# Matmul operands on multiples of 512 bytes, and a convolution tile without zero columns

## The chip, the cores and the metric

One NeuronCore of one Trainium2 chip runs the whole program. The metric is the device time of that core in microseconds (us), the median of the runs. TensorE (PE) multiplies, VectorE (DVE), ScalarE (ACT) and GpSimd (POOL) do the elementwise work, and SyncE (SP) issues the loads and stores. SBUF is the on-chip memory with 128 partitions; PSUM holds matmul results.

## What is computed

Two batches of 768 tokens go through three blocks, all in fp32. The first is a windowed attention with block summaries; the other two are dense. Cut to what matters here:

```python
# block 2: x is (2, 768, 512); w_in (512, 1024); w_spatial (768, 768)
h = np.maximum(x @ w_in, 0.0)
u, v = h[..., :512], h[..., 512:]
v_n = (v - mean(v)) / np.sqrt(var(v) + 1e-06)
v_s = np.einsum('ts,bsd->btd', w_spatial, v_n) + b_spatial[None, :, None]
x = (u * v_s) @ w_out                      # (2, 768, 512)
# block 3: w_in (512, 1024), conv_w (3, 1024), w_out (1024, 512)
h = np.maximum(x @ w_in, 0.0)
hp = zero_row, h, zero_row                 # along the 768 tokens
conv = sum(conv_w[k] * hp[:, k:k + 768, :] for k in range(3))
return (h * sigmoid(conv)) @ w_out
```

## The kernel before

Every dense product is made of fp32r parts: `split` (lines 66 to 73) writes a value as a high and a low half, and `mm3` (lines 58 to 64) adds up three matmuls for each 128 rows of the contraction: high by high (line 62), high by low (line 63) and low by high (line 64). In `PE.matmul` the first operand, `lhsT`, is the stationary one (128 columns, loaded into the array as weights), and `rhs` is the moving one (384 or 512 columns, streamed through).

After the attention, whose order is written out by a planner (`Plan`, lines 133 to 173), the dense stages follow each other (lines 610 to 620); there the framework's scheduler fixes the order on each engine when the program is built, from its own model of the times. Their tiles in the profile, in order:

- `f1v` (tile vps, 512 columns, 144 matmuls): stationary x, moving w1. `f1u` (ups, 384 columns): stationary w1, moving x.
- `spatial` (sps, 384 columns, 288 matmuls): stationary vn, moving wsp.
- `merge_weights` (wps, 512 columns, 96 matmuls): stationary wo, moving wi. It multiplies the two weight matrices between the blocks, once.
- `i2(b)` (hps, 384 columns, 192 matmuls for each batch b): stationary wp, moving g1. Its 8 steps f make h, the convolution and the gate.
- `o2(b)` (ops): stationary y, moving w2. For each batch 6 row tiles by 8 steps f by 3 matmuls, which makes 144. The last row tile of the second batch is done in two halves of 256 columns, so that 264 of the 288 have 512 columns and 48 have 256.

Where the operands lie: tiles are placed one after another in each partition, pool by pool, and every tile is rounded up to 32 bytes. The program's own constants and the pools `const` and `slots` end on a multiple of 512 bytes, and every tile of `slots` (w1, w2, wi, x, g1, vn, wp, u) begins on one. The pool `tmp` takes 5 tiles of 2048 bytes, 5 of 32 (bs) and 5 of 32 (mv): 10,560 bytes, which is 20 times 512 and 320 more. So the attention's pool and, after it in the same place, the pool `late` begin 320 bytes past a multiple of 512. In `late`, the 6 tiles of the tag S (6144 bytes, 12 times 512: wsp, later y) lie at 320; the 3 tiles of the tag T (line 604; 2 by 770 floats, 6160 bytes, placed 6176 apart) lie at 320, 352 and 384; the two Y tiles (y of f = 6 and 7) at 416. The stationary wo lies in T tiles (line 446, cut into units of 2048 bytes by `units`). So three kinds of dense operand lie off a multiple of 512: the moving wsp, the stationary wo and the stationary y.

The convolution (lines 476 to 497) works on one T tile for each f: in its first half hh, 770 columns wide, a zero column (DVE, lines 480 and 481), 768 columns of h that ACT writes from PSUM in two parts (line 486), and a zero column; in its second half ct. ACT writes the first tap (line 487), DVE adds the second and the third (line 489), ACT takes the sigmoid (line 490), POOL multiplies by h (line 491), and `split` writes y: its high half by ACT (line 70), its low half by POOL in batch 0 and by DVE in batch 1 (line 73). A T tile is free for step f + 3 when y of step f is written.

Of the kernel before, what the change touches and what calls it, by code (L numbers as in the profile page):

```python
# [11 lines left out]
F32 = mybir.dt.float32  # L12
F32R = mybir.dt.float32r
BF16 = mybir.dt.bfloat16
U32 = mybir.dt.uint32
AF = mybir.ActivationFunctionType
ALU = mybir.AluOpType
# [3 lines left out]
B, H, S, D = 2, 8, 768, 64  # L21
# [14 lines left out]
HS = S // 2  # L36
# [3 lines left out]
def block_kernel(ctx, tc, q_in, k_in, vwin, v_in, mask, runs, w_in, w_spT, b_sp, w_outT, w_in2, conv, w_out2, out):  # L40
    nc = tc.nc
    PE, DVE, ACT, POOL, SP = nc.tensor, nc.vector, nc.scalar, nc.gpsimd, nc.sync

    const = ctx.enter_context(tc.tile_pool(name="const", bufs=1))
    slots = ctx.enter_context(tc.tile_pool(name="slots", bufs=1))
    tmp = ctx.enter_context(tc.tile_pool(name="tmp", bufs=5))
    psm = ctx.enter_context(tc.tile_pool(name="psm", bufs=2, space=PSUM))

    mm_pools = [psm, None, 0]
# [2 lines left out]
    def mmps(name):  # L52
        mm_pools[2] += 1
        if mm_pools[1] and mm_pools[2] % 2:
            return mm_pools[1].tile([128, 512], F32, tag="o", name=name)
        return mm_pools[0].tile([128, 512], F32, tag="mm", name=name)

    def mm3(ps, pairs, first=True, last=True):

        n = len(pairs)  # L60
        for i, ((lh, ll), (rh, rl)) in enumerate(pairs):
            PE.matmul(ps, lhsT=lh, rhs=rh, start=first and i == 0, stop=False)  # L62
            PE.matmul(ps, lhsT=lh, rhs=rl, start=False, stop=False)  # L63
            PE.matmul(ps, lhsT=ll, rhs=rh, start=False, stop=last and i == n - 1)  # L64

    def split(src, hi, lo, heng=None, leng=None):

        heng, leng = heng or ACT, leng or POOL
        if heng is ACT:
            ACT.copy(hi, src)  # L70
        else:
            heng.tensor_copy(hi, src)
        leng.tensor_tensor(out=lo, in0=src, in1=hi.bitcast(F32), op=ALU.subtract)  # L73
# [40 lines left out]
    conv_t = const.tile([128, DF // 128 * 3], F32, name="conv_t")  # L114
# [213 lines left out]
    vn, u, g1, wsp = {}, {}, {}, []  # L328
# [92 lines left out]

    def load_wsp():
        for t in range(NT):
            wsp.append(late.tile([128, 2, S], F32R, tag="S", name=f"wsp_{t}", bufs=6))
            st = t_slot(f"wst_{t}", F32)[:, 0, :S]
            SP.dma_start(st, w_spT[t * 128:(t + 1) * 128, :])
            split(st, wsp[t][:, 0], wsp[t][:, 1], leng=POOL if t % 2 else DVE)
# [17 lines left out]
    def load_wo():  # L445
        wm["o"] = units(lambda n: t_slot(n, F32R), "wo", 8)
        for c in range(4):
            load_weight(w_outT[c * 128:(c + 1) * 128, :], wm["o"][2 * c], wm["o"][2 * c + 1], f"wot_{c}")
            yield
# [20 lines left out]
    def wp(c, hf):  # L470
        return wm["p"][8 * hf + 2 * c], wm["p"][8 * hf + 2 * c + 1]


    y, w2 = {}, {}

    def i2(b):
        for f in range(8):
            tt = t_slot(f"hh_{b}_{f}", F32)
            hh, ct = tt[:, 0], tt[:, 1, :S]
            DVE.memset(hh[:, 0:1], 0.0)  # L480
            DVE.memset(hh[:, S + 1:S + 2], 0.0)
            for h in range(2):
                ps = mmps(f"hps_{b}_{f}_{h}")
                fs, hs = slice(f % 4 * 128, (f % 4 + 1) * 128), slice(h * HS, (h + 1) * HS)
                mm3(ps[:, :HS], [((wp(c, f // 4)[0][:, fs], wp(c, f // 4)[1][:, fs]), (g1[b, c][:, 0, hs], g1[b, c][:, 1, hs])) for c in range(4)])
                ACT.activation(out=hh[:, 1 + h * HS:1 + (h + 1) * HS], in_=ps[:, :HS], func=AF.Relu)
            ACT.activation(out=ct, in_=hh[:, 0:S], func=AF.Copy, scale=conv_t[:, 3 * f:3 * f + 1])  # L487
            for j in (1, 2):
                DVE.scalar_tensor_tensor(out=ct, in0=hh[:, j:j + S], scalar=conv_t[:, 3 * f + j:3 * f + j + 1], in1=ct, op0=ALU.mult, op1=ALU.add)  # L489
            ACT.activation(out=ct, in_=ct, func=AF.Sigmoid)  # L490
            POOL.tensor_tensor(out=ct, in0=hh[:, 1:S + 1], in1=ct, op=ALU.mult)  # L491
            if f < 6:
                y[b, f] = late.tile([128, 2, S], F32R, tag="S", name=f"y_{b}_{f}", bufs=6)
            else:
                y[b, f] = late.tile([128, 2, S], F32R, tag="Y", name=f"y_{b}_{f}", bufs=2)
            split(ct, y[b, f][:, 0], y[b, f][:, 1], heng=ACT, leng=DVE if b else POOL)
            yield

# [99 lines left out]
    late = ctx.enter_context(tc.tile_pool(name="late", bufs=2))  # L598
# [2 lines left out]
    raw_pool[0] = late  # L601

    def t_slot(name, dt):
        return late.tile([128, 2, S + 2], dt, tag="T", name=name, bufs=3)

    b_bc = late.tile([128, S], F32, name="b_bc", bufs=1)
    SP.dma_start(b_bc, b_sp.partition_broadcast(128))
    load_wsp()
    load_f64(conv, "conv", conv_t)
    run(f1v(0))  # L610
# [4 lines left out]
    run(spatial(1), load_wi(1))  # L615
    run(merge_weights())
    run(i2(0), load_w2())
    run(o2(0))
    run(i2(1))
    run(o2(1))  # L620

# [57 lines left out]
```

## Time and profile before

| | |
|---|---|
| median of 3 runs | 360.98 us (360.39 to 361.37) |
| profiled execution: span from the first to the last instruction | 358.8 us |
| its own time | not given beside the span; the median lies 2.18 us above the span |
| busy PE, DVE, ACT, POOL | 345.1, 229.4, 183.4, 157.9 us |

The profile is one execution. Busy time is a union of the records on an engine; matmuls overlap in their records, so a busy PE need not be a PE at its peak. How fast PE works in a stage is better read from the starts of its matmuls: the time between the first start of a stage and the first start of the next, by the number of matmuls in between. That is called the pace below.

### The profile page before, as it was taken

The page shows a single profiled execution, that of the slowest core. Times are in us where ns is not written, and L with a number is a line of the kernel's source. Part 1 is how long each engine was busy: PE and PEld are TensorE (multiplying, and loading weights), DVE is VectorE, ACT ScalarE, POOL GpSimd, SP SyncE. Part 2 cuts the span into 40 slices and gives each one's busy share as a digit, 9 for nine tenths or more (in the row PEclk, how much of TensorE's full clock was granted, in tenths as well). Part 3 has the DMA queues.
Part 4 walks back from the last instruction along what each step waited for, and adds up shares of the span by engine and source line. Part 5 has one row for each costly group of instructions (what it writes and reads, how often), then busy time and mean ns, then how long its engine had stood idle before and what let it go on. Part 6 is the DMA issues. An engine that isn't in the chain of part 4 may idle for free.

```text
span 358.8 us, 6400 instructions
## 1 busy us (share of the span) xinstructions
PE 345.1 (96%) x2487; PEld 301.0 (84%) x2487; DVE 229.4 (64%) x390; ACT 183.4 (51%) x374; POOL 157.9 (44%) x159
## 2 busy tenths in 40 slices
PE   8998899999797999999999999999999999999996
PEld 4766677777586999899999888999888899998885
DVE  3889998884179799779298899457620025886000
ACT  2766778757264442355342464867531047874101
POOL 3789999765136142116133062587870003333000
PEclk9999999999899899999999999999999999999999
DMA  8877888320381232015232351000002020000202
GB/s 259 276 231 239 235 265 248 98 68 2 94 293 43 58 103 74 0 35 164 97 107 71 108 166 78 2 0 0 2 0 88 2 88 1 3 0 2 88 0 88
DMA packets 11118, 33.86 MB, mean 94 GB/s; under 512 B 1488, under 2 KB 1872, under 8 KB 11088
## 3 DMA queue, kind: packets, MB, share of 16 engines
q1 hardware_dynamic: 11088, 33.46, 29.8%
q8 instruction: 19, 0.31, 0.3%
q14 instruction: 11, 0.09, 0.1%
HBM read 30.31 MB, written 3.15 MB: 93 GB/s over the span
## 4 chain that ended last, share of the span: by engine, by line
PE 86%; DVE 4%; DMA 3%; POOL 2%; issue 2%; ACT 1%; SPq 0%; POOLq 0%; ACTq 0%; DVEq 0%
PE ops L63 6%; PE ops L62 6%; PE ops L64 6%; PE hps L62 6%; PE hps L63 6%; PE hps L64 6%; PE sps L64 5%; PE sps L62 5%; PE sps L63 5%; PE xp L310 3%; PE s L284 3%; PE pt L305 3%; PE mm L247 2%; PE vps L62 2%; PE wps L64 2%; PE wps L63 2%
## 5 line engine op out<-in xcount | busy, mean ns | idle before, releaser
L489 DVE SCALAR_TENSOR_TENSOR hh<-hh,conv_t 128x768 f32<-128x768 f32 x32 | 43.2, 1349 | 41.9 <-ACT hh L487 41.4
L491 POOL TENSOR_TENSOR hh<-hh 128x768 f32<-128x768 f32 x16 | 25.4, 1588 | 53.7 <-ACT hh L490 53.7
L63 PE MATMUL hps<-g,wp 128*128 128x384 f32 x128 | 42.8, 334 | 0.0
L64 PE MATMUL hps<-g,wp 128*128 128x384 f32 x128 | 42.8, 334 | 0.0
L62 PE MATMUL hps<-g,wp 128*128 128x384 f32 x128 | 42.8, 334 | 0.0
L62 PE MATMUL ops<-w,y 128*128 128x512 f32 (+1 forms) x104 | 39.0, 377 | 0.0
L63 PE MATMUL ops<-w,y 128*128 128x512 f32 (+1 forms) x104 | 38.9, 377 | 0.0
L64 PE MATMUL ops<-w,y 128*128 128x512 f32 (+1 forms) x104 | 37.8, 376 | 0.0
L62 PE MATMUL sps<-wsp,vn 128*128 128x384 f32 x96 | 32.9, 343 | 1.8 <-ACT vn L382 1.8
L64 PE MATMUL sps<-wsp,vn 128*128 128x384 f32 x96 | 32.7, 345 | 0.5 <-DVE vn L385 0.5
L63 PE MATMUL sps<-wsp,vn 128*128 128x384 f32 x96 | 32.9, 343 | 0.0
L301 POOL TENSOR_TENSOR e<-e,st 128x480 f32<-128x480 f32 x24 | 25.4, 1061 | 15.6 <-DVE st L298 5.3
L292 ACT ACTIVATE e<-s,st 128x120 f32<-128x120 f32 x96 | 26.8, 371 | 7.2 <-DVE st L288 7.1
L517 ACT COPY o<-ops 128x512 f32<-128x512 f32 (+1 forms) x13 | 6.8, 557 | 40.0 <-PE ops L64 39.5
L62 PEld LDWEIGHTS hps<-g,wp 128*128 128x128 f32 x128 | 24.0, 188 | 0.1
L63 PEld LDWEIGHTS hps<-g,wp 128*128 128x128 f32 x128 | 24.0, 188 | 0.1
L64 PEld LDWEIGHTS hps<-g,wp 128*128 128x128 f32 x128 | 24.0, 188 | 0.0
L64 PEld LDWEIGHTS ops<-w,y 128*128 128x128 f32 x104 | 19.5, 188 | 4.0
L62 PEld LDWEIGHTS ops<-w,y 128*128 128x128 f32 x104 | 19.5, 187 | 4.0
L63 PEld LDWEIGHTS ops<-w,y 128*128 128x128 f32 x104 | 19.5, 188 | 3.9
L73 POOL TENSOR_TENSOR wi<-wit_f,wi 128x512 fp32r<-128x512 f32 x8 | 12.8, 1604 | 20.4 <-ACT wi L70 20.4
L73 POOL TENSOR_TENSOR w<-w2t_f,w 128x512 fp32r<-128x512 f32 x8 | 11.9, 1519 | 20.5 <-ACT w L70 20.5
(121 smaller groups left out, 874.8 us busy)
## 6 DMA issues: line engine op xcount, KB each, us to landing
vw<-vwin SPq DMA_DIRECT2D x8, 576.0 KB, 5.5
raw<-w_in SPq DMA_DIRECT2D x8, 512.0 KB, 4.9
wit_raw<-w_in SPq DMA_DIRECT2D x8, 512.0 KB, 3.7
w2t_raw<-w_out SPq DMA_DIRECT2D x8, 512.0 KB, 3.7
kt<-k_in SPq DMA_DIRECT2D x8, 400.0 KB, 4.6
qt<-q_in SPq DMA_DIRECT2D x8, 384.0 KB, 3.6
out<-o SPq DMA_DIRECT2D x11, 256.0 KB, 2.0
wst<-w_spT SPq DMA_DIRECT2D x6, 384.0 KB, 4.9
```

Of the source, the lines that this page charges most:

```text
L62: PE.matmul(ps, lhsT=lh, rhs=rh, start=first and i == 0, stop=False)
L63: PE.matmul(ps, lhsT=lh, rhs=rl, start=False, stop=False)
L64: PE.matmul(ps, lhsT=ll, rhs=rh, start=False, stop=last and i == n - 1)
L73: leng.tensor_tensor(out=lo, in0=src, in1=hi.bitcast(F32), op=ALU.subtract)
L247: PE.matmul(ps, lhsT=runs_t[:, NZ - WK - 2 * blk:NZ - WK - 2 * blk + NK], rhs=vws[j][:WK, blk], start=blk == 0, stop=blk == NB - 1)
L284: PE.matmul(s[c * QB:(c + 1) * QB, h, a * NK:(a + 1) * NK], lhsT=qts[j][rows, blk * QB:(blk + 1) * QB], rhs=kws[j][rows, blk], start=False ...
L292: ACT.activation(out=e[:, u, :NK], in_=sv[:, u // 2, u % 2], func=AF.Exp, bias=st[:, 0, u:u + 1])
L301: POOL.tensor_tensor(out=e[:, :, :NK], in0=e[:, :, :NK], in1=st[:, 2].unsqueeze(2).to_broadcast([128, GB, NK]), op=ALU.mult)
L305: PE.transpose(pt[:, u], e[:, u, :NK], ident)
L310: PE.matmul(xp[h * D:(h + 1) * D, k * QB:(k + 1) * QB], lhsT=vws[j][:, g * GB + k, h * D:(h + 1) * D], rhs=pts[:, 2 * h + k // 2, k % 2 * ...
L489: DVE.scalar_tensor_tensor(out=ct, in0=hh[:, j:j + S], scalar=conv_t[:, 3 * f + j:3 * f + j + 1], in1=ct, op0=ALU.mult, op1=ALU.add)
L491: POOL.tensor_tensor(out=ct, in0=hh[:, 1:S + 1], in1=ct, op=ALU.mult)
```

## The change

A tile of 48 floats (192 bytes) is added to `tmp`, and nothing uses it: the pool then takes 21 times 512 bytes. The T tile loses its two extra columns (6144 bytes). The tag S gets 8 tiles, and the two Y tiles go: y of all f lies in S tiles. With that wsp, wo and y begin on multiples of 512; the attention's tiles move by 192 bytes, and none of the dense operands that lay on a multiple before leaves it. In the convolution the zero columns and their two memsets go, h begins at column 0, ACT writes the middle tap over all 768 columns first, and DVE adds the other two taps over 767 columns each, shifted by one column against h.

```diff
     tmp = ctx.enter_context(tc.tile_pool(name="tmp", bufs=5))
+    tmp.tile([128, 48], F32, tag="pad", name="pad", bufs=1)
...
-            wsp.append(late.tile([128, 2, S], F32R, tag="S", name=f"wsp_{t}", bufs=6))
+            wsp.append(late.tile([128, 2, S], F32R, tag="S", name=f"wsp_{t}", bufs=8))
...
-            hh, ct = tt[:, 0], tt[:, 1, :S]
-            DVE.memset(hh[:, 0:1], 0.0)
-            DVE.memset(hh[:, S + 1:S + 2], 0.0)
+            hh, ct = tt[:, 0], tt[:, 1]
...
-                ACT.activation(out=hh[:, 1 + h * HS:1 + (h + 1) * HS], in_=ps[:, :HS], func=AF.Relu)
-            ACT.activation(out=ct, in_=hh[:, 0:S], func=AF.Copy, scale=conv_t[:, 3 * f:3 * f + 1])
-            for j in (1, 2):
-                DVE.scalar_tensor_tensor(out=ct, in0=hh[:, j:j + S], scalar=conv_t[:, 3 * f + j:3 * f + j + 1], in1=ct, op0=ALU.mult, op1=ALU.add)
+                ACT.activation(out=hh[:, h * HS:(h + 1) * HS], in_=ps[:, :HS], func=AF.Relu)
+            ACT.activation(out=ct, in_=hh, func=AF.Copy, scale=conv_t[:, 3 * f + 1:3 * f + 2])
+            for j, to, of in ((0, slice(1, S), slice(0, S - 1)), (2, slice(0, S - 1), slice(1, S))):
+                DVE.scalar_tensor_tensor(out=ct[:, to], in0=hh[:, of], scalar=conv_t[:, 3 * f + j:3 * f + j + 1], in1=ct[:, to], op0=ALU.mult, op1=ALU.add)
             ACT.activation(out=ct, in_=ct, func=AF.Sigmoid)
-            POOL.tensor_tensor(out=ct, in0=hh[:, 1:S + 1], in1=ct, op=ALU.mult)
-            if f < 6:
-                y[b, f] = late.tile([128, 2, S], F32R, tag="S", name=f"y_{b}_{f}", bufs=6)
-            else:
-                y[b, f] = late.tile([128, 2, S], F32R, tag="Y", name=f"y_{b}_{f}", bufs=2)
+            POOL.tensor_tensor(out=ct, in0=hh, in1=ct, op=ALU.mult)
+            y[b, f] = late.tile([128, 2, S], F32R, tag="S", name=f"y_{b}_{f}", bufs=8)
...
-        return late.tile([128, 2, S + 2], dt, tag="T", name=name, bufs=3)
+        return late.tile([128, 2, S], dt, tag="T", name=name, bufs=3)
```

## Rows read from the trace of the kernel before

**Rows 1.** The page's part 1: busy us, share of the span, instructions.

```profile
PE 345.1 (96%) x2487; PEld 301.0 (84%) x2487; DVE 229.4 (64%) x390; ACT 183.4 (51%) x374; POOL 157.9 (44%) x159
```

**Rows 2.** The page's part 4: the chain that ended last, by engine.

```profile
PE 86%; DVE 4%; DMA 3%; POOL 2%; issue 2%; ACT 1%; SPq 0%; POOLq 0%; ACTq 0%; DVEq 0%
```

**Rows 3.** Windows: length; busy PE, PEld, DVE, ACT, POOL; PE clock; DMA share, rate.

```profile
112.00:119.50 7.50, 5.23 (x21) 4.55 (x20) 6.98 (x17) 3.23 (x6) 5.57 (x5) 0.79 0.00 0
...
119.50:355.20 235.70, 235.70 (x1230) 216.54 (x1228) 139.55 (x220) 108.64 (x178) 77.25 (x50) 1.00 0.16 51
...
221.30:254.50 33.20, 33.20 (x193) 33.16 (x192) 21.23 (x32) 24.60 (x38) 23.36 (x14) 1.00 0.00 1
254.50:288.00 33.50, 33.50 (x146) 27.02 (x145) 6.08 (x12) 9.18 (x15) 12.28 (x7) 1.00 0.06 24
...
333.00:347.00 14.00, 14.00 (x62) 11.28 (x61) 0.00 (x0) 1.76 (x3) 0.00 (x0) 1.00 0.15 56
```

**Rows 4.** Timeline of PE: the first matmul of each stage (start us, length us).

```profile
141.23 0.39 PE L62 MATMUL vps<-w,x 128*128 128x512 f32 x1
...
157.57 0.33 PE L62 MATMUL ups<-x,w 128*128 128x384 f32 x1
...
174.23 0.33 PE L62 MATMUL sps<-wsp,vn 128*128 128x384 f32 x1
...
199.19 0.39 PE L62 MATMUL wps<-wi,wo 128*128 128x512 f32 x1
...
221.42 0.34 PE L62 MATMUL hps<-g,wp 128*128 128x384 f32 x1
...
254.71 0.39 PE L62 MATMUL ops<-w,y 128*128 128x512 f32 x1
...
288.25 0.34 PE L62 MATMUL hps<-g,wp 128*128 128x384 f32 x1
```

**Rows 5.** Groups of PE in five windows, from 144, 200, 255, 333 and 122 us.

```profile
L62 PE MATMUL vps<-w,x 128*128 128x512 f32 x20 | 7.8, 389 | 0.0
...
L62 PE MATMUL wps<-wi,wo 128*128 128x512 f32 x29 | 11.4, 393 | 0.0
...
L62 PE MATMUL ops<-w,y 128*128 128x512 f32 x47 | 18.4, 394 | 0.0
...
L62 PE MATMUL ops<-w,y 128*128 128x512 f32 x21 | 8.3, 395 | 0.0
...
L62 PE MATMUL sps<-wsp,vn 128*128 128x384 f32 x33 | 11.1, 336 | 0.0
```

**Rows 6.** The same view over the whole span: aligned hps, and an attention matmul.

```profile
L62 PE MATMUL hps<-g,wp 128*128 128x384 f32 x128 | 42.8, 334 | 0.0
...
L310 PE MATMUL xp<-pts,vw 120*64 120x64 f32 x384 | 16.4, 228 | 3.4 <-ACT pts L322 1.9 <-DVE st L298 1.5
```

**Rows 7.** Waits of SP from 80 us on: us in total, times, longest.

```profile
SPq L607 <- PE xp L310: 20.4, 1, 20.4
```

**Rows 8.** Groups of the span: one zero column's memset, and the taps.

```profile
L480 DVE MEMSET hh<- 128x1 f32 x16 | 0.9, 59 | 11.6 <-POOL y L73 11.3
...
L489 DVE SCALAR_TENSOR_TENSOR hh<-hh,conv_t 128x768 f32<-128x768 f32 x32 | 43.2, 1349 | 41.9 <-ACT hh L487 41.4
```

**Rows 9.** Timelines of DVE and ACT in one step of `i2(0)`.

```profile
237.93 1.02 DVE L489 SCALAR_TENSOR_TENSOR hh<-hh,conv_t 128x768 f32<-128x768 f32 x1
...
240.69 3.04 DVE L489 SCALAR_TENSOR_TENSOR hh<-hh,conv_t 128x768 f32<-128x768 f32 x2 [0.20 <-ACT hh L487]
...
243.76 0.85 ACT L490 ACTIVATE hh<-hh 128x768 f32<-128x768 f32 x1 [0.64 <-DVE hh L489]
244.51 0.92 ACT L487 ACTIVATE hh<-hh,conv_t 128x768 f32<-128x768 f32 x1
```

**Rows 10.** Timelines in `o2(0)`: y of f = 4, PE's first use.

```profile
255.46 2.22 POOL L73 TENSOR_TENSOR y<-hh,y 128x768 fp32r<-128x768 f32 x1
...
257.51 0.63 PE L62 MATMUL ops<-w,y 128*128 128x512 f32 x2
```

## The prediction

> **What bounds the kernel now.** I began with the page's busy times: PE is busy 96% of the span and no other engine over 64% [rows 1]. The reader should see that this alone proves little, since records of matmuls overlap. So the next view is the chain of waits: 86% of what ended last is PE itself, and the rest is spread over the attention and the start of the dense part [rows 2]. Third, the windows: from 119.5 to 355.2 us PE has no idle time at all, at a granted clock of 1.00; just ahead, from 112 to 119.5 us, PE idles 2.3 us and the clock reads 0.79 [rows 3]. So from there to the end only the pace of the matmuls counts, and an engine beside PE counts only where it makes PE wait.
>
> The pace is then read from the first starts of the stages [rows 4]. vps: (157.57 - 141.23) / 72 = 226.9 ns. sps: (199.19 - 174.23) / 144 = 173.3 ns. wps: (221.42 - 199.19) / 96 = 231.6 ns. hps: (254.71 - 221.42) / 192 = 173.4 ns. ops: (288.25 - 254.71) / 144 = 232.9 ns. Three stages have the same form, 128 by 128 by 512 columns, and two of them are slower than the third by 4.7 and 6.0 ns. By the tile sizes these are the two whose stationary operand lies off a multiple of 512 bytes; the moving operands of all three lie on one. The lengths of the single records say the same: 389 ns in vps, 393 in wps, 394 in ops [rows 5].
>
> Is it the neighbours' work? In `o2(0)` DVE, ACT and POOL are busy for 6.1, 9.2 and 12.3 of 33.5 us [rows 3], and from 333 to 347 us DVE and POOL do nothing and ACT 1.8 of 14 us [rows 3], while the mean is still 395 [rows 5]. So contention does not explain it. sps, whose moving operand lies off, has records 2 ns longer than hps (336 against 334) [rows 5, 6], but the same pace: a moving operand at 384 columns costs nothing that can be seen.
>
> **The change, part by part.**
> *ops.* 264 matmuls of 512 columns. If an aligned y gives them the pace of vps, the nearest row with the same form, that is 264 x 6.0 = 1.58 us. The 48 of 256 columns have no aligned row of their width; between 0 and the same 6.0 ns (0.29 us) I take 0, as the 384-column stage hid its shift.
> *wps.* 96 x 4.7 = 0.45 us in the same way. All of it lies on the path, as PE has no idle time there.
> *sps.* 288 matmuls, 0: their pace is already that of the aligned hps.
> Together 2.03 us; the bounds are 0 (the excess has another cause) and 2.3 us (with the 256-column ones).
>
> *The wait for y.* A faster ops reads y earlier. In `i2(0)` y comes late: the low half of y for f = 4 ends on POOL at 255.46 + 2.22 = 257.68, and PE's first use of it, the 14th matmul of the stage, starts at 257.51 + 0.23 = 257.74 [rows 10]. That is 0.06 us of slack. The 13 matmuls ahead of it save 13 x 6.0 = 0.08 us, so 0.02 us is given back there. What comes before `i2(0)`, the gain in wps, moves h, y and PE alike.
>
> *The convolution.* 32 memsets of 59 ns go [rows 8]: 1.9 us of DVE, hidden, as DVE is busy for 21.2 of 33.2 us in `i2(0)` [rows 3] and PE waits for no memset; without that cover it would be the whole 1.9. Their waits for a free T tile (11.3 us in all [rows 8]) pass to ACT's first write of h. Behind that write on ACT stand the sigmoid and the copy of y of the steps before, for which POOL waits; but in the kernel before ACT's write needs the same free tile, so nothing waits that did not, and DVE is freed. The taps: 32 DVE instructions of 1349 ns on average [rows 8] over 767 columns in place of 768, unchanged to 0.2%. Their operands change places: before, h was read one or two floats past its start and ct was whole; now one tap writes ct one float past its start. No row shows what that costs. The rows bound it: a single tap took 1.02 us, and two in a row 3.04 [rows 9], so 1.02 and 3.04 - 1.02 = 2.02, 0.3 us less to 0.7 us more than the mean for each; I take 0, as both taps already read with a shift. ACT's middle tap has the size of the first tap. POOL's product loses its shift of one float; 0.
>
> *The two new S tiles, and the attention.* y of f = 0 and 1 now take tiles that no wsp used; nothing waited there. The first load of the pool `late` waits for the attention's last matmul as a whole (SP's wait of 20.4 us ends on xp [rows 7]), so new addresses free nothing earlier. The attention's operands move by 192 bytes, and none of them gets onto a multiple of 512 by plan; blocks of 256 bytes straddle one in half the cases before and after. I take 0. As a bound, 2 ns (the moving-operand excess above) on each of the commonest group, 384 matmuls [rows 6]: 0.8 us either way.
>
> *The sum.* 358.8 - 2.03 + 0.02 = 356.8 us (356.79) of span. The median of the runs stands 2.18 us above the span of the profiled execution; with that, **359.0 us**, 0.55% under 360.98. A measurement of this kernel can tell about 0.3% (1.1 us) from no change.
>
> **The rivals.**
> *No effect: about 361.0 us.* The excess of wps and ops could come from something they share other than the placement. For it: the shift of wsp costs sps no pace, and the excess differs (4.7 and 6.0 ns). Against it: two stages, with different neighbours, agree. It would also come out so if the added tile did not shift the pools as the sizes say.
> The Trainium skill ("Advanced Engine Details and Errata", SBUF Cachelines) says that SBUF works in lines of 16 bytes and that accesses run at full rate while they stay in a line; by that rule, as all these offsets are multiples of 32, the change would do nothing. By it the sum would be 0, and the rows of wps and ops speak against it as the only rule.
>
> *Slower: the taps in `i2(0)`, 362.1 us or more.* A step f there takes a loop longer than the 24 x 173.4 ns = 4.16 us that PE needs for it: two taps from 240.69 on (3.04 us), the sigmoid behind them, and behind that on ACT the next step's first tap, which ends at 244.51 + 0.92 = 245.43 and on which the next taps wait: 4.74 us [rows 9]. That loop has no slack, and y of f = 4 has 0.06 us [rows 10]. If each tap takes d longer for its shifted write, y of f = 4, the fifth step, comes 10d later, and PE waits for nearly all of it. With d = 0.31 us PE loses 3.1 us, and 359.0 becomes 362.1. The point from which it decides: at d = 0.1 us it eats half of the gain, at 0.2 us all of it, at 0.31 the kernel is slower by what can be measured. For it: no free DVE time in the loop, and an unaligned write is new. Against it: taps were read with shifts before, and still one took 1.02 us.
>
> *More gain: a clock stretch goes, 357.4 us.* From 112 to 119.5 us the granted clock is 0.79 on average [rows 3], between the levels 1.2 and 2.4 GHz: 0.42 x 7.5 = 3.2 us at the lower one, after PE had idled; at the upper one 1.6 us would be saved. The change touches nothing ahead of it but the attention's addresses, so only chance could move it.
>
> *Partly eaten: about 360.3 us.* The framework's scheduler orders the instructions anew, and an order that fits y worse, or the attention's shift, takes about 1.3 us of the 2.0.
>
> **How the numbers follow.** Forecast 0.62 (its own range 358.2 to 359.8); no effect 0.15; taps slower 0.10; clock 0.06; partly eaten 0.07. Faster by over 0.3%: 0.62 + 0.06 = 0.68. Within: 0.15 + 0.07 = 0.22. Slower: 0.10. The range from 357.8 to 361.4 holds the forecast, no effect and the partly eaten case, 0.84, and leaves out the clock and the slow taps.
>
> **What the changed profile would show.** Right: ops and wps records of 389 ns in place of 394 and 393, a pace of 227 ns in both, hps, sps and vps as before, no memset, o2(0) shorter by 0.8 us. Wrong: ops stays at 394 with y aligned (no effect); or ops falls to 389, but PE shows idle time ahead of ops on POOL's y, with two taps over 3.4 us (the slow rival); or a window about 112 to 119.5 us with a clock of 1.00.

## The result: slower, and the profile after

The changed kernel takes 363.37 us (median of 17 runs, 360.90 to 366.42); the kernel before, run as often on the same chip, 360.98 (359.03 to 367.14). The ratio is 1.006, with a 95% interval of 1.004 to 1.008. Some runs are slow, by about 1.5% or more; medians and ranges have them in, the ratios leave them out. The forecast was 359.0 and faster, so it was wrong in its sign: the gain that it worked out is there, and something that it priced at 0 costs more.

The profiled execution of the changed kernel took 363.39 us, with a span of 361.6 (358.8 before). First the busy times and the shares of the chain of waits, which answer to [rows 1, 2].

```profile
PE 344.0 (95%) x2487; PEld 301.6 (83%) x2487; DVE 234.9 (65%) x358; ACT 183.0 (51%) x374; POOL 165.0 (46%) x159
...
PE 62%; DVE 18%; DMA 6%; ACT 5%; issue 4%; POOL 2%; SPq 1%; ACTq 0%; DVEq 0%; POOLq 0%
```

DVE has 32 instructions fewer, the memsets, and yet is busy 5.5 us longer; POOL has the same 159 and is busy 7.1 us longer. The chain, 86% PE before, now leaves PE and runs over DVE. That is the first sign of where to look. Next the groups of PE in the windows from 200 and from 270 us, against [rows 5].

```profile
L63 PE MATMUL wps<-wi,wo 128*128 128x512 f32 x30 | 11.7, 389 | 0.0
...
L63 PE MATMUL ops<-w,y 128*128 128x512 f32 x29 | 11.3, 389 | 0.0
```

Both stages have the 389 ns of the aligned vps, as forecast (393 and 394 before). Then the timeline of PE (start us, length us): the first matmuls of the stages, against [rows 4], and what happens inside `o2(0)`.

```profile
199.51 0.39 PE L63 MATMUL wps<-wi,wo 128*128 128x512 f32 x1
...
221.32 0.33 PE L63 MATMUL hps<-g,wp 128*128 128x384 f32 x1
...
254.62 0.39 PE L63 MATMUL ops<-w,y 128*128 128x512 f32 x1
...
257.38 0.39 PE L63 MATMUL ops<-w,y 128*128 128x512 f32 x1
259.96 0.50 PE L63 MATMUL ops<-w,y 128*128 128x512 f32 x1 [2.19 <-ACT y L71]
...
261.46 0.63 PE L64 MATMUL ops<-w,y 128*128 128x512 f32 x1
...
264.40 0.40 PE L63 MATMUL ops<-w,y 128*128 128x512 f32 x1
...
291.46 0.33 PE L63 MATMUL hps<-g,wp 128*128 128x384 f32 x1
...
324.77 0.39 PE L63 MATMUL ops<-w,y 128*128 128x512 f32 x1
```

From the first starts: wps takes 21.81 us (22.23 before), `i2(0)` 33.30 (33.29), **`o2(0)` 36.84 (33.54)**, `i2(1)` 33.31 (33.30). The last `o2` takes 33.17 to the end of its matmuls (33.73). Everything up to vps came 0.3 us later, and the tail is 0.1 us longer. So one stage holds the whole loss: 3.3 us, or 4.16 against the 32.68 us that `o2(0)` takes with aligned operands and no wait (shown below). Of the 4.16, one wait is 259.96 - 257.38 - 0.23 = 2.35 us, for ACT's copy of y; behind it the matmuls start every 0.43 us in place of 0.23, until 264.40. The window of that stretch (columns as in [rows 3]) shows why:

```profile
260.90:264.30 3.40, 3.40 (x10) 2.63 (x9) 2.62 (x2) 0.87 (x2) 3.40 (x2) 0.50 0.00 0
```

The granted clock reads 0.50, the lower of the two levels (1.2 of 2.4 GHz), right after PE stood still. By the starts PE loses 1.6 us there: 3.64 us for the nine matmuls from 260.76 to 264.40, which take 2.04 at 0.227 each. The rest, 0.2 us, is small gaps. How much shorter the stage would be without this stretch is another question; the section on the table load comes back to it.

**Why y came late.** The y that PE waits for is that of f = 4. Its copy by ACT starts at 259.09; in the kernel before it started at 254.57, 4.52 us earlier. Timelines of ACT, first after, then before:

```profile
230.32 1.28 ACT L489 ACT_TABLE_LOAD   x1 [2.04 <-DVE hh L488]
...
257.51 0.84 ACT L489 ACTIVATE hh<-hh 128x768 f32<-128x768 f32 x1 [2.52 <-DVE hh L488]
...
259.09 0.82 ACT L71 CAST y<-hh 128x768 fp32r<-128x768 f32 x1
```

```profile
228.38 1.28 ACT L490 ACT_TABLE_LOAD   x1
...
252.99 0.85 ACT L490 ACTIVATE hh<-hh 128x768 f32<-128x768 f32 x1 [1.75 <-DVE hh L481]
...
254.57 1.76 ACT L70 CAST y<-hh 128x768 fp32r<-128x768 f32 x2
```

And of POOL (the product, line 490 after and 491 before, and the low half of y), after and before:

```profile
232.53 1.85 POOL L490 TENSOR_TENSOR hh<-hh 128x768 f32<-128x768 f32 x1 [4.17 <-ACT hh L489]
235.33 2.63 POOL L74 TENSOR_TENSOR y<-hh,y 128x768 fp32r<-128x768 f32 x1 [0.95 <-ACT y L71]
...
254.04 2.56 POOL L490 TENSOR_TENSOR hh<-hh 128x768 f32<-128x768 f32 x1
...
273.39 1.84 POOL L74 TENSOR_TENSOR y<-hh,y 128x768 fp32r<-128x768 f32 x1 [0.94 <-ACT y L71]
```

```profile
230.75 1.54 POOL L491 TENSOR_TENSOR hh<-hh 128x768 f32<-128x768 f32 x1 [2.83 <-ACT hh L490]
...
238.02 2.33 POOL L73 TENSOR_TENSOR y<-hh,y 128x768 fp32r<-128x768 f32 x1 [0.95 <-ACT y L70]
...
249.88 2.26 POOL L491 TENSOR_TENSOR hh<-hh 128x768 f32<-128x768 f32 x1
...
267.13 1.55 POOL L73 TENSOR_TENSOR y<-hh,y 128x768 fp32r<-128x768 f32 x1 [0.94 <-ACT y L70]
```

Two things changed. First, both POOL instructions take 0.30 us longer at the same size: the product 1.84 in place of 1.54, the low half 1.84 in place of 1.55 where nothing runs beside it (f = 7, the last rows) and 2.63 in place of 2.33 beside a tap on DVE. POOL does a product, waits 0.95 us for ACT's copy, does the low half, and goes on with the next product without a pause, so its step grows by two times 0.30: from (249.88 - 230.75) / 4 = 4.78 to (254.04 - 232.53) / 4 = 5.38 us. Second, the first product starts 1.78 us later. Of that, 1.34 us is POOL's longer idle time ahead of it, 4.17 in place of 2.83: ACT's table load for the sigmoid, 1.28 us, runs behind the taps (its row ends in a wait for DVE) where before it ran beside them. The other 0.45 us is there because the taps of f = 0 end that much later (230.24, 229.79 before), beside POOL's work on w2, which is late by as much. The two things make up the delay: 1.78 + 4 x 0.60 + 0.30 for the product of f = 4 itself = 4.48 of 4.52 us.

The last link to the copy is not that product, though. On ACT the copy of f = 4 comes behind the sigmoid of f = 5 (the rows at 257.51 and 252.99), which waits for DVE's taps of f = 5; in the kernel before the row names the memset right behind them. These taps run beside POOL's low half of f = 3 and its product of f = 4, and they end 4.47 us later than before (257.42, 252.95). So POOL's delay reaches the copy through DVE and ACT, and that is the DVE of the chain above.

DVE's group has the same sign and hides the agent: the taps' mean went from 1349 [rows 8] to 1556 ns.

```profile
L488 DVE SCALAR_TENSOR_TENSOR hh<-hh,conv_t 128x767 f32<-128x767 f32 x32 | 49.7, 1556 | 52.9 <-ACT hh L486 52.4
```

A tap by itself still takes 1.02 us, in both kernels; what grew is a tap that runs beside a POOL instruction (in `i2(0)` the first of a pair, about 2.0 us before and 2.5 after).

### The profile page after: what moved, and what is told of

Same layout as the page of the kernel before. It is cut to its first block, busy times and chain, and to the rows that moved or that the text cites. A ratio compares the mean times of both kernels' runs of the same rounds, so it can differ in the third digit from the quotient of the medians.

```text
span 361.6 us, 6394 instructions
## 1 busy us (share of the span) xinstructions
PE 344.0 (95%) x2487; PEld 301.6 (83%) x2487; DVE 234.9 (65%) x358; ACT 183.0 (51%) x374; POOL 165.0 (46%) x159
## 4 chain that ended last, share of the span: by engine, by line
PE 62%; DVE 18%; DMA 6%; ACT 5%; issue 4%; POOL 2%; SPq 1%; ACTq 0%; DVEq 0%; POOLq 0%
PE ops L65 6%; PE ops L63 6%; PE ops L64 6%; DVE hh L488 6%; PE hps L65 3%; PE sps L63 3%; PE hps L63 3%; PE hps L64 3%; PE sps L65 3%; DMA w2t_raw<-w_out 3%; PE sps L64 3%; PE xp L311 3%; PE s L285 3%; PE pt L306 2%; PE vps L63 2%
## 5 line engine op out<-in xcount | busy, mean ns | idle before, releaser
L488 DVE SCALAR_TENSOR_TENSOR hh<-hh,conv_t 128x767 f32<-128x767 f32 x32 | 49.7, 1556 | 52.9 <-ACT hh L486 52.4
L490 POOL TENSOR_TENSOR hh<-hh 128x768 f32<-128x768 f32 x16 | 30.2, 1886 | 52.1 <-ACT hh L489 52.1
L63 PE MATMUL ops<-w,y 128*128 128x512 f32 (+1 forms) x104 | 39.6, 381 | 2.2 <-ACT y L71 2.2
L64 PE MATMUL ops<-w,y 128*128 128x512 f32 (+1 forms) x104 | 39.0, 378 | 0.0
L65 PE MATMUL ops<-w,y 128*128 128x512 f32 (+1 forms) x104 | 38.3, 380 | 0.0
L63 PE MATMUL sps<-wsp,vn 128*128 128x384 f32 x96 | 33.5, 349 | 1.8 <-ACT vn L383 1.8
L65 PE MATMUL sps<-wsp,vn 128*128 128x384 f32 x96 | 32.9, 347 | 1.8 <-DVE mv L375 1.8
L64 PE MATMUL sps<-wsp,vn 128*128 128x384 f32 x96 | 33.2, 346 | 0.0
L63 PEld LDWEIGHTS ops<-w,y 128*128 128x128 f32 x104 | 20.0, 192 | 6.2 <-ACT y L71 2.6
L65 PEld LDWEIGHTS ops<-w,y 128*128 128x128 f32 x104 | 19.9, 192 | 3.7 <-POOL y L74 0.2
L64 PEld LDWEIGHTS ops<-w,y 128*128 128x128 f32 x104 | 19.9, 191 | 3.6
L74 POOL TENSOR_TENSOR y<-hh,y 128x768 fp32r<-128x768 f32 x8 | 20.0, 2509 | 5.7 <-ACT y L71 5.7
```

Of the source, the lines that this page charges most:

```text
L488: DVE.scalar_tensor_tensor(out=ct[:, to], in0=hh[:, of], scalar=conv_t[:, 3 * f + j:3 * f + j + 1], in1=ct[:, to], op0=ALU.mult, op1=ALU.add)
L490: POOL.tensor_tensor(out=ct, in0=hh, in1=ct, op=ALU.mult)
```

## The experiments

In the expectations P is the theory that POOL's product and subtraction became slower with the new places of their inputs, and that this makes y late. Its rivals there put the loss into the other half of the change, the places of the dense operands and tiles (A), or into the taps (T). The last three runs weigh P alone against P with the table load (L). All ratios are against runs of the kernel before on the same chip. The table shows what was read from each profile: POOL's product; the low half of y with nothing beside it; POOL's step in `i2(0)` (from the first product to the fifth, by 4); from the first hps to the first product; the length of `o2(0)`; and the ratio of the times. Each profile is one execution, but the stages repeat: `i2(0)` takes 33.29 to 33.31 us in all twelve.

| kernel | product us | low half | step | first product | o2(0) us | ratio (95%) |
|---|---|---|---|---|---|---|
| before | 1.54 | 1.55 | 4.78 | 9.33 | 33.54 | 1 |
| changed | 1.84 | 1.84 | 5.38 | 11.21 | 36.84 | 1.006 (1.004 to 1.008) |
| conv_only | 1.85 | 1.85 | 5.38 | 10.51 | 36.73 | 1.010 (1.006 to 1.014) |
| align_only | 1.54 | 1.55 | 4.78 | 9.88 | 32.68 | 0.995 (0.992 to 0.999) |
| shift8 | 1.54 | 1.54 | 4.78 | 11.29 | 33.31 | 0.995 (0.992 to 0.999) |
| shift12 | 1.84 | 1.55 | 5.08 | 11.20 | 34.78 | 1.003 (0.999 to 1.007) |
| shift4 | 1.54 | 1.83 | 5.09 | 11.24 | 34.88 | 1.001 (0.998 to 1.003) |
| ylo_dve | 1.84 | on DVE | 4.76 | 11.09 | 34.09 | 0.997 (0.994 to 1.000) |
| shift8_dve | 1.54 | on DVE | 4.47 | 11.25 | 32.68 | 0.995 (0.990 to 0.999) |
| align_slow | 1.84 | 1.84 | 5.38 | 9.82 | 35.41 | 1.001 (0.998 to 1.005) |
| after_table | 1.84 | 1.84 | 5.38 | 9.90 | 35.59 | 1.003 (0.999 to 1.008) |
| s8_table | 1.54 | 1.54 | 4.78 | 9.87 | 32.68 | 0.998 (0.994 to 1.002) |

### The two halves by themselves

conv_only has the new convolution and its T tile, and the old places of the dense operands. Against the changed kernel:

```diff
-    tmp.tile([128, 48], F32, tag="pad", name="pad", bufs=1)
...
-            wsp.append(late.tile([128, 2, S], F32R, tag="S", name=f"wsp_{t}", bufs=8))
+            wsp.append(late.tile([128, 2, S], F32R, tag="S", name=f"wsp_{t}", bufs=6))
...
-            y[b, f] = late.tile([128, 2, S], F32R, tag="S", name=f"y_{b}_{f}", bufs=8)
+            if f < 6:
+                y[b, f] = late.tile([128, 2, S], F32R, tag="S", name=f"y_{b}_{f}", bufs=6)
+            else:
+                y[b, f] = late.tile([128, 2, S], F32R, tag="Y", name=f"y_{b}_{f}", bufs=2)
```

> The convolution of the changed kernel (no zero columns, middle tap first, both halves of the T tile at the same place within 512 bytes), with the operands of before (no added tile, y at 320 and 416, wo off a multiple too). Theory P (POOL's two-input instructions are slower when both inputs begin at the same place): POOL's product takes 1.84 us as in the changed kernel, y's low half alone 1.84, a step of i2(0) 5.4 us, PE waits over 2 us for y at the start of o2(0), ops keep 394 ns; about 365 us, 2 us over the changed kernel. Theory T (the shifted taps are what costs): the same time, but POOL's product back at 1.54 us once the alignment of the pools is undone, as the taps alone lengthen. Theory A (the cost comes from the alignment of the pools, not from the tile): product 1.54, no wait, about 361 us.

Measured: 363.71 against 361.27 us. The groups of the span, and the waits of PE from 200 us on (us in total, times, longest):

```profile
L489 POOL TENSOR_TENSOR hh<-hh 128x768 f32<-128x768 f32 x16 | 30.2, 1888 | 52.6 <-ACT hh L488 52.6
```

```profile
PE ops L62 <- ACT y L70: 1.4, 1, 1.4
PE ops L64 <- POOL y L73: 0.6, 2, 0.4
```

The product is slow with the operands in their old places, and PE waits for y, with ops at the unaligned 395 ns. By the starts the first wait is 1.6 us, where over 2 were expected, and three shorter ones follow. The ratio of 1.010 is not told apart from the changed kernel's 1.006. So the convolution's half brings the loss, and the alignment has no part in it.

align_only has the aligned operands with the convolution of before: zero columns, memsets, T tiles of S + 2. So that wo lies on a multiple too, it takes S tiles in place of T tiles (one of the three stays in T). Against the changed kernel, with the convolution's lines as in the kernel before:

```diff
-        wm["o"] = units(lambda n: t_slot(n, F32R), "wo", 8)
+        wm["o"] = units(wo_slot, "wo", 8)
...
-        return late.tile([128, 2, S], dt, tag="T", name=name, bufs=3)
+        return late.tile([128, 2, S + 2], dt, tag="T", name=name, bufs=3)
+
+    def wo_slot(n):
+        return t_slot(n, F32R) if n == "wo_2" else late.tile([128, 2, S], F32R, tag="S", name=n, bufs=8)
```

> The operands of the changed kernel (added tile, eight S tiles; wo in two S tiles and one T tile, so that it is aligned too), with the convolution tile of before: zero columns, h from column 1, first tap first, ct 3080 bytes behind hh. Theory P: product 1.54 us, step of i2(0) 4.8, ops and wps at 389 ns and a pace of 227 ns, no wait over 0.3 us, no stretch of low clock in o2(0): about 359 us. Theory T: the same. Theory A: product 1.84 and a wait at the start of o2(0), about 363 us.

Measured: 359.07 against 361.27 us, 1.7 us less by the ratio. PE waits for nothing in `o2`, and ops has 389 ns:

```profile
L63 PE MATMUL ops<-w,y 128*128 128x512 f32 x88 | 34.1, 389 | 0.0
```

By the stages it gains 0.43 us in wps, 0.86 in `o2(0)` and 0.55 in `o2(1)`, 1.84 together. That is the forecast's first half alone, 2.03 us but for 0.2. With conv_only it also accounts for the result: -0.5% and +1.0%.

### One distance changed: shift8

The changed kernel, but ct is placed 8 bytes further from h; no zero column, no memset, the middle tap first. (`wo_slot` as above keeps wo aligned.)

```diff
-            hh, ct = tt[:, 0], tt[:, 1]
+            hh, ct = tt[:, 0, :S], tt[:, 1, :S]
...
-        return late.tile([128, 2, S], dt, tag="T", name=name, bufs=3)
+        return late.tile([128, 2, S + 2], dt, tag="T", name=name, bufs=3)
```

> The changed kernel with two more columns in each half of the T tile, so that ct begins 3080 bytes behind hh in place of 3072, that is 8 bytes off; wo as in the kernel before this one, aligned; taps and their order as in the changed kernel. Theory P: product back to 1.54 us and y's low half alone to 1.55, taps as before, step 4.8 us, no wait for y over 0.3 us, ops at 389 ns: about 359 us. Theory T: taps stay as in the changed kernel (first of a pair about 2.46 us), step about 5.4, wait over 2 us, about 363 us.

Measured: 359.55 against 361.27 us. Timeline of POOL:

```profile
237.43 1.54 POOL L490 TENSOR_TENSOR hh<-hh 128x768 f32<-128x768 f32 x1
239.92 2.33 POOL L74 TENSOR_TENSOR y<-hh,y 128x768 fp32r<-128x768 f32 x1 [0.95 <-ACT y L71]
```

Eight bytes bring both POOL instructions back to their old times, and the kernel to the time of align_only. One short wait is left, for ACT's copy of f = 7, so that `o2(0)` takes 33.31 us and not 32.68; s8_table below removes it. The taps write with the same shift as in the changed kernel, so the forecast's slow rival, the taps, is out; and the missing memsets are worth nothing that can be measured, which is what the forecast said of them.

### The map of distances: offsets_pool

A kernel of POOL instructions alone (then of taps on DVE alone): the same product on two tiles that begin on multiples of 512, with the inputs shifted by whole floats; it leaves out the attention and all matmuls.

```python
    for _ in range(3):
        POOL.tensor_tensor(out=o[:, :S], in0=a[:, 0:0 + S], in1=b[:, 1:1 + S], op=ALU.mult)
```

> No attention and no dense product: POOL alone, then DVE alone. POOL multiplies two tiles of 128 by 768 with the inputs at chosen offsets (bytes past a multiple of 512), three times each; then subtracts; DVE does the tap form with both inputs at 0,0 / 4,8 / 8,8 / 0,4 / 4,0. Theory P: POOL about 1.84 us where both inputs begin at the same place modulo some small number of bytes (0,0 and 8,8), about 1.54 us where they are 4 or 8 bytes apart; larger steps (16, 32, 64, 256) show which number it is. DVE 1.02 us in all five. Theory T: DVE longer by 0.2 us or more at 0,4 and 4,0, POOL the same everywhere.

Measured, by the groups; the second input begins 0 (line 59), 4 (61), 8 (63), 12 (65) and 16 (67) bytes behind the first, and in line 81 both begin 8 bytes past a multiple of 512:

```profile
L59 POOL TENSOR_TENSOR o<-a,b 128x768 f32<-128x768 f32 x3 | 5.4, 1801 | 3.9 <-DVE o L54 3.7
...
L61 POOL TENSOR_TENSOR o<-a,b 128x768 f32<-128x768 f32 x3 | 4.6, 1545 | 0.2
L63 POOL TENSOR_TENSOR o<-a,b 128x768 f32<-128x768 f32 x3 | 4.6, 1545 | 0.2
...
L65 POOL TENSOR_TENSOR o<-a,b 128x768 f32<-128x768 f32 x3 | 5.4, 1802 | 0.2
...
L67 POOL TENSOR_TENSOR o<-a,b 128x768 f32<-128x768 f32 x3 | 5.4, 1802 | 0.2
...
L81 POOL TENSOR_TENSOR o<-a,b 128x768 f32<-128x768 f32 x3 | 5.4, 1803 | 0.2
```

There are two levels and nothing between. As far as tried, only the distance between the inputs counts, not where each begins: with (second minus first) modulo 16 equal to 4 or 8 it takes 1.54 us, with 0 or 12 it takes 1.80. Distances of 32, 64, 128 and 256 gave 1.80, 264 gave 1.54, and the subtraction has the same two levels. The taps took 1.02 us at all five placements tried. In the changed kernel ct begins 3072 bytes behind h and y's halves on multiples of 512: 0 modulo 16 for both instructions. In the kernel before h began 4 bytes into the tile and ct 3080: 4 modulo 16 for the product, and 8 for the low half. The zero column and the tile of 770 floats had kept the two apart by chance.

### The map tried in the kernel: shift12 and shift4

shift8 with T tiles of S + 3 and of S + 1 in place of S + 2. By the map, S + 3 (3084 bytes) gives 12 for the product and 4 for the low half; S + 1 (3076) gives 4 and 12: each makes one of the two slow.

```diff
-        return late.tile([128, 2, S + 2], dt, tag="T", name=name, bufs=3)
+        return late.tile([128, 2, S + 3], dt, tag="T", name=name, bufs=3)
```

> As shift8, but with three more columns in each half of the T tile, so that ct begins 3084 bytes behind hh: 12 past a multiple of 16. Theory P, as the POOL runs alone have it (slow where the second input begins 0 or 12 bytes past the first modulo 16, fast at 4 and 8): POOL's product (hh, then ct) 1.84 us, y's low half (ct, then y) at 4 and so 1.55 us alone; a step of i2(0) 5.08 us, half way between; PE waits about 1 us for y in o2(0); 360 to 361 us. If any shift at all were enough: product 1.54, step 4.78, 359 us.

> As shift8, but with one more column in each half: ct 3076 bytes behind hh, 4 past a multiple of 16. Theory P: product 1.54 us, y's low half (ct, then y: 12 modulo 16) 1.84 us alone; step 5.08 us, PE waits about 1 us; 360 to 361 us, like shift12. If any shift were enough: 1.54 and 1.55, step 4.78, 359 us.

Measured: the one that the map names is slow in each, 1.84 or 1.83 us, and the other is fast (the table). The step is 5.08 and 5.09 us, half way between 4.78 and 5.38, and `o2(0)`, 34.78 and 34.88 us, is 2.1 and 2.2 us over align_only, half of the 4.16. The times, 362.16 and 361.19 against 361.32 us, lie between shift8 and the changed kernel, but only just: shift12 is over the 361 us expected, and its interval overlaps that of the changed kernel, as shift4's overlaps that of shift8. The wait of PE ahead of y of f = 4 comes back in part (shift12, then shift4, which also waits 0.4 us for POOL's low half):

```profile
PE ops L63 <- ACT y L71: 1.0, 1, 1.0
```

```profile
PE ops L63 <- ACT y L71: 0.8, 1, 0.8
```

### Half of POOL's work moved: ylo_dve and shift8_dve

The low half of y goes to DVE in both batches, first in the changed kernel, then in shift8.

```diff
-            split(ct, y[b, f][:, 0], y[b, f][:, 1], heng=ACT, leng=DVE if b else POOL)
+            split(ct, y[b, f][:, 0], y[b, f][:, 1], heng=ACT, leng=DVE)
```

> The changed kernel with y's low half of batch 0 on DVE, as in batch 1; POOL keeps only the slow product, 1.84 us. Theory P with POOL's serial chain (product, ACT's copy, low half) as what sets the step: the chain is cut, a step of i2(0) falls to 4.9 us or less, PE waits under 0.3 us, about 359 us. If DVE's taps set the step by themselves: DVE gets 0.95 us more in each step, step 5.4 us or more, wait over 2 us, 363 us or more.

> shift8 with y's low half of batch 0 on DVE: all dense operands aligned, the fast POOL product, and POOL's serial chain cut. Theory P: product 1.54 us; shift8 waited 0.5 us in o2(0) in its profile, this should wait 0.3 us or less if the chain was still the bound there; 358.8 to 359.5 us, a ratio to the kernel before of about 0.995, the best so far or equal to shift8. If DVE, with 0.95 us more in each step, becomes the bound of the step: more wait than in shift8, 360 us.

Measured: ylo_dve 360.44 against 361.32 us. The step falls to 4.76 us with the product still at 1.84, and the long wait goes. Two waits for DVE's low half take its place:

```profile
PE ops L65 <- DVE y L74: 0.8, 2, 0.4
```

So moving the work buys back most of the loss, but the slow product still costs 1.4 us of `o2(0)`, more than expected. shift8_dve has no wait and 32.68 us there, the same as align_only: it adds nothing to shift8 in the time (361.71 against 361.94 us on a chip whose runs of the kernel before went from 359.89 to 365.27).

### Which placement slows PE: offsets_pe

A kernel of matmuls alone, in chains of 48 with the weights loaded for each, the stationary or the moving operand so many bytes past a multiple of 512; nothing else is computed.

> PE alone, no attention and no product of the kernel: chains of 48 matmuls of the fp32r form, weights loaded anew for each. 512 columns with the stationary operand 0, 32, 64, 128, 256, 320, 384 and 416 bytes past a multiple of 512 and the moving one at 0; then moving at 320; then 384 and 256 columns with the stationary one at 0, 320 and 416; then 384 columns with the moving one at 320. If the placement of the stationary operand sets the pace: 227 ns at 0, 229 to 235 at the others with 512 columns, 227 with the moving one at 320; 173.3 at 384 columns and moving 320. If the excess belonged to the neighbours in wps and ops: 227 ns throughout. At 256 columns the changed kernel went from 116 to 120 ns: 120 at 0 and 116 at 320 if that too comes from the stationary one.

Measured, on the timeline of PE; the stationary operand lies at 0 (line 59), 32 (62), 128 (68), 256 (71), 320 (74), and in line 83 at 0 with the moving one at 320:

```profile
19.72 11.05 PE L59 MATMUL ps<-m,w 128*128 128x512 f32 x48
30.61 11.35 PE L62 MATMUL ps<-m,w 128*128 128x512 f32 x48
41.80 11.36 PE L65 MATMUL ps<-m,w 128*128 128x512 f32 x48
53.00 11.32 PE L68 MATMUL ps<-m,w 128*128 128x512 f32 x48
64.16 11.05 PE L71 MATMUL ps<-m,w 128*128 128x512 f32 x48
75.04 11.36 PE L74 MATMUL ps<-m,w 128*128 128x512 f32 x48
...
108.59 11.16 PE L83 MATMUL ps<-m,w 128*128 128x512 f32 x48
119.59 8.49 PE L86 MATMUL ps<-m,w 128*128 128x384 f32 x48
```

A pace is the distance of two starts by 48: (30.61 - 19.72) / 48 = 226.9 ns at 0, 233.1 at 32, 232.5 at 128, 226.7 at 256. So a multiple of 256 bytes is enough for the stationary operand, and the other places tried cost 6 ns (64, 320, 384 and 416 as well). With the moving operand at 320 the pace is (119.59 - 108.59) / 48 = 229.2 ns, 2.3 more. With 384 columns a stationary operand at 320 costs 3.2 ns (176.7 against 173.5), a moving one nothing. With 256 columns there is no such loss: 119.6 at 0, 117.9 at 320, 119.8 at 416, where 116 was expected at 320.

### The table load: align_slow, after_table, s8_table

align_slow is align_only with T tiles of S + 3 and ct two floats in, which makes both POOL instructions slow while the table load stays where it was before. (The expectation misstates the bytes: h begins at 4 and ct at 3092, which is 0 modulo 16 for the product and 12 for the low half. Both are slow distances.)

```diff
-            hh, ct = tt[:, 0], tt[:, 1, :S]
+            hh, ct = tt[:, 0], tt[:, 1, 2:S + 2]
...
-        return late.tile([128, 2, S + 2], dt, tag="T", name=name, bufs=3)
+        return late.tile([128, 2, S + 3], dt, tag="T", name=name, bufs=3)
```

> The convolution of the kernel before (zero columns, memsets), dense operands on multiples of 512, and T tiles in which ct begins 3088 bytes behind tile start and h 4 bytes behind it, so that POOL's product and y's low half both have their second input 12 bytes past the first modulo 16. Two theories for the late y of f = 4 in the changed kernel. P alone: the two longer POOL instructions do it all; then the steps are 5.38 us, as there, and PE waits about 2.2 us in o2(0), which lasts 36 us or more. P and L: a second cause is that ACT's table load ahead of the first sigmoid waits for DVE's taps in the changed kernel (1.28 us on the path at f = 0), and in the kernel before it ran while the taps ran; then here, where the first product starts as early as before, four steps of 0.60 and a product of 0.30 make y of f = 4 some 2.7 us later, against about 2.2 us between its copy and PE's use in the kernel before: a wait of 0.3 to 0.8 us, o2(0) of 33.0 to 34.0 us. POOL's idle time ahead of the first product 2.8 us, not 4.2.

after_table is the changed kernel, and s8_table is shift8, with a sigmoid of one column (its result is not used), so that ACT loads its table beside the taps:

```diff
-    tmp.tile([128, 48], F32, tag="pad", name="pad", bufs=1)
+    pad = tmp.tile([128, 48], F32, tag="pad", name="pad", bufs=1)
...
                 ACT.activation(out=hh[:, h * HS:(h + 1) * HS], in_=ps[:, :HS], func=AF.Relu)
+                if (b, f, h) == (0, 1, 0):
+                    ACT.activation(out=pad[:, 0:1], in_=hh[:, 0:1], func=AF.Sigmoid)
```

> The changed kernel with one sigmoid of a single column on ACT behind the first half of h of f = 1, so that the table is loaded while DVE works on the taps of f = 0. P alone: nothing changes, PE waits about 2.2 us for ACT's copy of y, o2(0) stays at 35 us or more. P and L: POOL's idle time ahead of its first product falls from 4.2 to about 2.9 us, everything behind it comes 1.3 us earlier, PE's wait falls to 0.7 to 1.1 us, o2(0) to 33.5 to 34.5 us; the time falls by 1 to 2 us against the changed kernel, a ratio of about 1.000 against the kernel before.

> shift8 with the same early sigmoid: both causes undone, no memsets. P alone: o2(0) stays at 33.3 us as in shift8. P and L: o2(0) falls to 32.7 us, as in align_only, with no wait of PE, and the ratio against the kernel before is 0.993 to 0.997.

Measured: 362.18, 362.31 and 359.72 against 361.51 us. In after_table the table load starts at 227.59, right behind the relu, and POOL's first product waits 2.82 us as in the kernel before:

```profile
227.59 1.28 ACT L487 ACT_TABLE_LOAD   x1
...
230.52 1.85 POOL L492 TENSOR_TENSOR hh<-hh 128x768 f32<-128x768 f32 x1 [2.82 <-ACT hh L491]
```

The waits of PE in after_table; those of align_slow are 0.7, and 0.7 in two, and in s8_table there is none.

```profile
PE ops L63 <- ACT y L71: 0.9, 1, 0.9
PE ops L65 <- POOL y L74: 0.7, 2, 0.4
```

The first wait is near what P and L expected, 0.7 and 0.9 in place of 2.2 us: the table load is a cause of that wait. But `o2(0)` lasts 35.4 and 35.6 us, over a microsecond more than expected. PE now waits at four places: at the 14th matmul for ACT's copy of f = 4, and at the 25th, 33rd and 54th for the low halves of f = 4, 5 and 6. By the starts that is 2.6 and 2.8 us in all, where the changed kernel waited 2.45 us at one place. So the slow POOL instructions alone bring about two thirds of the 4.16 us.

The length of the stage is set by the last of these places. Here is the low half of f = 6 and the 54th matmul, first in the changed kernel, then in after_table:

```profile
268.02 2.62 POOL L74 TENSOR_TENSOR y<-hh,y 128x768 fp32r<-128x768 f32 x1 [0.95 <-ACT y L71]
...
270.78 0.65 PE L65 MATMUL ops<-w,y 128*128 128x512 f32 x2
```

```profile
266.05 2.61 POOL L74 TENSOR_TENSOR y<-hh,y 128x768 fp32r<-128x768 f32 x1 [0.95 <-ACT y L71]
...
268.71 0.74 PE L65 MATMUL ops<-w,y 128*128 128x512 f32 x2 [0.30 <-POOL y L74]
```

In after_table PE starts 0.05 us after the low half has landed. In the changed kernel, whose stage began at 254.62, the low half landed at 270.64 and PE was there 0.14 us later, without a wait. From the 54th matmul to the end of the stage it is 20.8 us in after_table and 20.7 here. So, by one execution of each, the low clock cost the stage 0.1 us at most: at full clock PE would have come to the 25th, 33rd and 54th matmul earlier and waited there, by an estimate from the landings (8.12, 10.64 and 16.02 us into the stage) and 0.227 us for each matmul about 1.3 us in all. conv_only, which has no such stretch, loses 3.2 us to waits alone (36.73 against 33.54). What the changed kernel has beyond after_table, 36.84 - 35.59 = 1.25 us, is then the table load, which makes POOL's first product 1.31 us later (11.21 against 9.90).

By the stages, then, the table load adds the 1 to 2 us expected. The times do not confirm it: 1.003 (0.999 to 1.008) against 1.006 (1.004 to 1.008) is not told apart. With fast POOL instructions it costs less: `o2(0)` 33.31 us in shift8, 32.68 in s8_table, so 0.6 us of the stage, which the times (0.995 and 0.998, intervals that overlap) don't resolve; 0.998 is also just above the 0.993 to 0.997 expected.

**Faster than both kernels:** align_only, shift8 and shift8_dve, all at 0.995 with intervals below 1.

## Why the prediction was wrong, step by step

- **The bound and the pace: right.** The excess of wps and ops was the stationary operand's place. wps gave 0.42 us (0.45 forecast), `o2(0)` 0.86 us where nothing waits (144 x 6.0 = 0.86). Over 264 matmuls the term of 1.58 stands. Why the excess of wps was 4.7 ns and not 6.0 stays open. The rival "no effect" is out. The Trainium skill ("Advanced Engine Details and Errata", SBUF Cachelines), by whose lines of 16 bytes all these places would be equal, does not describe the stationary operand: 32, 64 and 128 bytes off cost 6 ns in offsets_pe, 256 costs none.
- **The 256-column matmuls: 0 forecast, a loss measured.** By their starts the 42 that follow each other without a break went from 116.5 to 119.8 ns, which is about 0.16 us for the 48. The bounds (0 to 0.29 gain) excluded a loss without a reason.
- **"POOL's product loses its shift of one float; 0": the step that failed.** It was the one step with no bounds, although its operands moved as the taps' did, and y's low half, whose input ct moved too, was not named at all. They cost 0.30 us each, 0.60 in each step, and by that alone `o2(0)` grew from 32.68 to 35.41 us, 2.7 us (align_only, align_slow). A row of the kernel before would have bounded it: the low halves of wsp on POOL, a subtraction of the same size whose inputs both lie on multiples of 16 bytes, took 1.85 us and more there, against 1.54 for the product.
- **The slack of y of f = 4: misread, to the safe side.** The forecast gave it 0.06 us, from POOL's low half against the 14th matmul. But [rows 10] show two matmuls of line 62 in a row there, high by high, and line 62 does not read the low half. What the 14th waits for is ACT's copy, which ended at 254.57 + 0.82 = 255.39 before (0.82 us is one copy); it had 257.74 - 255.39 = 2.35 us. Of the 4.52 us that the copy was later, 2.35 were absorbed. PE came 0.17 us earlier, and so waited 2.35. The low half of f = 4 is first waited for at the 25th matmul.
- **A wait was added, and not seen.** The forecast looked for new waits at the T tiles alone ("nothing waits that did not"). In the instruction lists of the two kernels the first sigmoid waited for DVE alone before; now it waits for DVE and for ACT's own earlier write, and the first of the two waits stands on the table load ahead of it, so 1.28 us came onto the path of the first step, worth 1.25 us of `o2(0)`. That two taps of 767 columns no longer cover what ACT's middle tap wrote explains the second wait; this is argued from the code, while the place of the load is in the trace, and moving it was tried.
- **The slower rival: right place, wrong agent.** It said that the step of `i2(0)` has no slack, that a longer step makes y of f = 4 late and that PE then waits, 3.1 us at 0.31 us for each tap. The step grew by 0.60, PE waited 2.35, and even its sign was there, two taps over 3.4 us (3.51), though PE waited for ACT's copy and not for POOL. But the taps were the victims: 1.02 us alone, at every placement tried. POOL's two instructions were the agents. The chance of 0.10 on one agent was too low for a mechanism that any of four instructions could set off.
- **Memsets 0, taps 0, sps 0: right** (without memsets s8_table has the 32.68 us of align_only in `o2(0)`; shift8's taps; sps 24.95 us, 24.96 before).
- **The clock near 112 us: as said, it did not go,** and a second stretch came, in `o2(0)`, which no case had. That the clock fell behind a wait of 2.35 us is shown in one execution; conv_only and shift12, with waits of 1.6 and 1.1 us there, kept 0.23 us. What decides it was not tried and stays open. The stage was hardly longer for it.
- **The sum.** Forecast 358.8 - 2.0 = 356.8 of span. Measured: 358.8 - 1.8 for the pace, + 4.2 for the late y in `o2(0)`, + 0.4 of small differences ahead and behind = 361.6. Of the 4.2, 2.7 to 2.9 are the slow POOL instructions (align_slow, after_table) and about 1.3 the table load. The forecast's 2.18 us between span and time were 1.8 in the changed kernel.

## What to carry to other kernels

When a change moves a tile by a few bytes, list every instruction that reads it, on every engine, and ask of each two-input instruction how its inputs now lie to each other; making everything round can be what costs. Look in the old trace for another instruction of the same form at the new placement before a step is priced at 0. And check which half of a value a matmul reads, and which instruction carries a new second wait, before a slack is put in numbers. Where PE waits several times in a stage, look for the last of the waits before you add up the losses: a slow stretch ahead of it may only take the place of waiting.

## What the runs showed of the hardware that was not expected

- POOL's product and subtraction of two fp32 inputs (128 by 768) take 1.54 us when the second input begins 4 or 8 bytes past the first modulo 16, and 1.80 at 0 or 12; the absolute places tried don't matter. Why 12 goes with 0 stays open.
- DVE's tap of the same size takes 1.02 us at all five placements tried; it grows only beside POOL (in `i2(0)` about 2.0 us beside a product of 1.54, 2.5 beside one of 1.84), as POOL's low half grows beside a tap (1.55 to 2.33).
- TensorE's pace in 512 columns with weights loaded for each matmul is 226.7 to 226.9 ns with the stationary operand on a multiple of 256 bytes and 232.5 to 233.3 off it; at 256 columns the order is not the same (119.6 at 0, 117.9 at 320), which stays unexplained.
- ACT's table load, 1.28 us, can stand behind a wait that belongs to the instruction it is loaded for.
